# A gated attention and a MoE on one core: the MoE's second product in plain float32, with new groups, buffers and stream times

## The chip, the cores and the metric

The kernel runs on one core of one Trainium2 chip. Its engines work side by side, each through its own queue in order: PE (matrix products; PEld is its weight loads), DVE (VectorE), ACT (ScalarE), POOL (GpSimd) and SP, which here issues the DMAs. The metric is the device time of one execution in microseconds, lower is better.

## What is computed

A recurrence with a complex decay, per batch and head, and then a two-layer MoE-like block on its output, all in float32:

```python
for t in range(S):                       # S = 768, D = 48, B = 4, H = 8
    new_re = ar * S_re - ai * S_im
    new_im = ar * S_im + ai * S_re
    S_re, S_im = new_re + k[t] v[t]^T, new_im
    y[t] = q[t] @ S_re
x = y laid out as (3072 tokens, 384)
h = x @ w_in                             # (384, 2048)
g = h * clip(h + 3, 0, 6) / 6
out = g @ w_out                          # (2048, 384)
```

## The kernel before

The sequence is cut into 24 chunks of 128 tokens (six per batch). The attention works chunk by chunk, the MoE in groups of chunks.

- `normal` and `chain` turn the decays of three chunks (one *chain*, 8 in all) into cumulative products. This is DVE work almost alone: L350 to L352 and L384 to L388. The tile `z` holds a chain; `cw` carries the factors between chunks, by DMA.
- `prep(cc)` makes one chunk's scaled q and k: ACT squares, logarithm and exponential (L463 to L467), two products on POOL or, for the first chains, on DVE (L465 and L469, `E = V if CHAINS[q][0] < PV else P`), then L470, L471 and four products into the tile `gg` (L477). Six DMAs (L488) turn `gg` into the tile `kq`.
- `mat(cc)` is the chunk's part on PE: `pA` (L509, masked into `am` by DVE, L510), `py` (L522, in four column tiles of the array, once with `am` and once with the running `state`), the transposes `pt` (L538), the state's update `pG` (L552), and the split of `py` into two float32r parts `xh` and `xl` (L563, L564). These float32 products appear in the page as two records each.
- `moe(g)` runs over the 16 slices `f` of the 2048 hidden columns. A round is: 9 matmuls (L609) into the PSUM tile `ph` (2 buffers); ACT makes `r` (L612); DVE makes the gated value and puts it back in `ph` (L614); ACT copies it as float32r into `gh` (L616); DVE puts the remainder into `gl` (L618); and LAG = 2 rounds later `second` does three float32r matmuls per chunk of the group (L597 to L599) into `po`. A group has three chunks, so a round has 9 + 9 matmuls of 384 columns.
- `weights(f)` brings the weights, which lie in memory as 64-bit floats, one part at a time (w_in, then w_out): a DMA into `ws` (L258), ACT shifts the low word (L264), DVE puts the words together (L267, L268), ACT copies the float32r part (L271), POOL subtracts for the remainder (L272). So both weights stand in the SBUF as two float32r tiles.
- `weights_guard` loads the weights again for a check of their size (three ACT activations each, L283 to L286, 32 of them); its tile shares the two buffers of `sq` in `normal`. Its result is used only after the last group.

Each of these is a generator, and a *stream* says when its pieces stand in the program: a start and an end on a made-up axis in which a chunk of MoE takes 16/3. The table `PAR` holds the numbers; a heap takes the stream with the lowest time next, and that, with a scheduler behind it, sets the order on every engine. The lines that decide the groups and the buffers are

```python
F1='VPVVVV', CP=16, SZ='33333333', CS='3.3.3.3.3.3.3.3', NV=1,
GGB, SQB, ZB, XB, WTB, LAG, RB, EX, AS, OV, KQB = 1,2,2,2,2,2,2,0,1,1,2
```

Of the kernel before, what the change touches and what calls it, by code (L numbers as in the profile page):

```python
# [21 lines left out]
C = 128  # L22
HALF = 64
NFF = 16
NB = 8
BL = HALF // NB

PITCH = HALF + 4
AT = 4
CHAIN_PIECES = BL - 1 + 3 + 2 + 1  # L30

PAR = dict(
    W0=-140.37, W1=0.5, CE=0.82, CL=15.36, PL=-0.12, ML=6.47, PD=6.7, C0=-162.25, L0=9.13, A0=-152.93,
    D0=6.25, P0=-1.45, M0=-98.58, C1=-122.4, L1=37.46, A1=-131.86, D1=9.53, P1=34.72, G0=134.98, G1=0.29,
    NL=6.55, ND=3.47, NP=1.37, CH=6.71, AO=-0.82, GA=19.17, GB=-1.42, N1=-42.6, N2=3, PV=2, F0='VVVVVV',
    F1='VPVVVV', CP=16, SZ='33333333', CS='3.3.3.3.3.3.3.3', NV=1,
)
# [12 lines left out]
CHAINS, CHUNK, LAST = [], [], []  # L50
# [5 lines left out]
COLS = [2 * q for q in range(len(CHAINS) + 1)]  # L56
# [146 lines left out]
def tile_gated_attention_moe(ctx, tc, aL, GL, vL, wL, maskL, qkvaL, out):  # L203
# [28 lines left out]
    n64 = wp.tile([C, 18], F32, name="n64")  # L232
# [8 lines left out]
    wout_h = wp.tile([C, NFF, DM], F32R, name="wout_h")  # L241
    wout_l = wp.tile([C, NFF, DM], F32R, name="wout_l")
# [4 lines left out]
    def weights(f):  # L247

        for part in range(2):
            while GA + GB * (2 * f + part) > 0 and 0 not in CWs:  # L250
                yield "wait"
            st = pa.tile([C, DM], I64, tag="sq" if WTB == 0 else "ws", name="ws", bufs=WTB or SQB)
            at = GA + GB * (2 * f + part)
            if at > 0:

                i = AT + int(min(at / 2, BL - 1)) * NB
                P.tensor_copy(st.bitcast(F32)[0:1, 0:1], Z[0][0:1, 0, 0, i : i + 1])
            SP.dma_start(out=st, in_=wL[:, f, part])  # L258
            words = st.bitcast(I32).rearrange("p (n two) -> p n two", two=2)
            low, high = words[..., 0], words[..., 1]  # L260
            if AS:

                ulow = st.bitcast(mybir.dt.uint32).rearrange("p (n two) -> p n two", two=2)[..., 0]
                A.activation(low, ulow, AF.Copy, scale=2.0**-29 * (1 - 2.0**-18), bias=7.5 * 2.0**-18 - 0.5)  # L264
            else:
                V.tensor_scalar(low, low, 29, None, ALU.logical_shift_right)
            V.scalar_tensor_tensor(low, high, 3, low, ALU.logical_shift_left, ALU.bitwise_or)  # L267
            V.scalar_tensor_tensor(low, high, 0x3FFFFFFF, low, ALU.bitwise_or, ALU.bitwise_and)  # L268
            w = st.bitcast(F32).rearrange("p (n two) -> p n two", two=2)[..., 0]
            hi, lo = (win_h, win_l) if part == 0 else (wout_h, wout_l)  # L270
            A.activation(hi[:, f], w, AF.Copy)  # L271
            P.tensor_tensor(lo[:, f], w, hi[:, f], ALU.subtract)  # L272
            if part:
                WEIGHTS.add(f)
            yield
# [16 lines left out]
    CWs = {}  # L292

    def normal(q, f):


        zt, n, first = CHAINS[q]
        w = 6 * n
# [33 lines left out]
        if f:  # L332
            V.tensor_tensor(at, at, m2.unsqueeze(1).to_broadcast([C, 2, 3 * n, HALF]), ALU.mult)
# [3 lines left out]
        NORMAL.add((q, f))  # L337
        yield

    def chain(q):  # L340
# [19 lines left out]
        while (q, 0) not in NORMAL or (q, 1) not in NORMAL:  # L360
            yield "wait"
# [17 lines left out]
        zs = z[:, :, :, AT : AT + HALF - NB].rearrange("p k x (i b) -> p k x i b", b=NB)[..., 1:]  # L379
        fac = e[..., : NB - 1].unsqueeze(3)  # L380
        shape = [C, w, BL - 1, NB - 1]
        fx = pa.tile([C, 2, *shape[1:]], F32, tag="fx", name="fx", bufs=1)
        for k in range(2):
            V.tensor_tensor(fx[:, k], zs[:, k], fac[:, 1].to_broadcast(shape), ALU.mult)  # L384
# [197 lines left out]
    def moe(g):  # L582
# [11 lines left out]
        def second(f, gh, gl):  # L594
            for i in range(n):
                ts = slice(i * C, (i + 1) * C)
                T.matmul(po[i], gl[:, ts], wout_h[:, f], start=f == 0, stop=False)  # L597
                T.matmul(po[i], gh[:, ts], wout_l[:, f], start=False, stop=False)  # L598
                T.matmul(po[i], gh[:, ts], wout_h[:, f], start=False, stop=f == NFF - 1)  # L599

        late = []
        for f in range(NFF):
# [10 lines left out]

            V.scalar_tensor_tensor(ph, r, 1.0, ph, ALU.min, ALU.mult)  # L614
            gh = pg.tile([C, C * n], F32R, tag="gh", name="gh", bufs=LAG + 1)
            A.activation(gh, ph, AF.Copy)  # L616
            gl = pg.tile([C, C * n], F32R, tag="gl", name="gl", bufs=LAG + 1)
            V.tensor_tensor(gl, ph, gh, ALU.subtract)  # L618
            late.append((f, gh, gl))
# [15 lines left out]
    def stream(make, start, end, pieces):  # L635
        streams.append([start, len(streams), (end - start) / pieces, make, None])
# [6 lines left out]
    for q, (t, n, first) in enumerate(CHAINS):  # L643
# [7 lines left out]
        stream(lambda q=q: chain(q), a, b, CHAIN_PIECES)  # L651
        for f in range(2):
            at = a - p["NL"] + f * p["ND"] * n / 3
            stream(lambda q=q, f=f: normal(q, f), at, at + p["NP"], 3)
# [139 lines left out]
```

## Time and profile before

| | us |
|---|---|
| median of 3 runs | 813.24 (812.2 to 815.07) |
| the profiled execution | 810.45 |
| its span, first to last instruction | 808.7 |
| PE busy | 626.4 (77%) |
| DVE busy | 543.5 (67%) |
| ACT busy | 367.7 (45%) |
| POOL busy | 222.4 (28%) |

PE's busy time counts records that overlap, so it isn't PE at its peak. The span in 40 equal slices (each digit the busy share in tenths; PEclk the granted TensorE clock in tenths; about 20 us a slice):

```profile
PE   0002857877637789978998989879998999999994
DVE  3986966889998659888967885777535442432332
PEclk9999997969767789989999999989997999999997
```

PE has nothing to do in the first three slices and half of the fourth, where the first chain and the first `kq` are made. DVE is nearly full in the first half and under half full in the last quarter, where the attention has ended and MoE alone runs.

### The profile page before, as it was taken

To read this page: it belongs to the slowest core of one execution; us is meant where nothing else is said; L and a number is where in the kernel's file an instruction comes from. 1 tells how busy PE (TensorE), PEld (TensorE's weight loads), DVE (VectorE), ACT (ScalarE), POOL (GpSimd) and SP (SyncE) were. 2 spreads that over 40 slices of the span, in tenths; PEclk is the share of its full clock that TensorE was granted. 3 is DMA by queue.
4 is the path that set the end of the run, shared out by engine and by line. 5 is a ranking of instruction groups with operands and counts; after the bars stand their busy time and mean duration, and the time that the engine had idled before them with its cause. 6 is when DMAs were issued, how large, how long until landed. Compare 5 with 4: busy or idle time off the path is not lost.

```text
span 808.7 us, 12677 instructions
## 1 busy us (share of the span) xinstructions
PE 626.4 (77%) x4577; PEld 573.5 (71%) x4577; DVE 543.5 (67%) x1063; ACT 367.7 (45%) x785; POOL 222.4 (28%) x220
## 2 busy tenths in 40 slices
PE   0002857877637789978998989879998999999994
PEld 0002647766527688867997788778887899988994
DVE  3986966889998659888967885777535442432332
ACT  6241225535433353353337335577687743333331
POOL 4254445335532432252125232413101100000000
PEclk9999997969767789989999999989997999999997
DMA  5116628527135454445332443465678440100000
GB/s 195 33 46 139 159 70 222 120 64 192 59 85 104 102 133 93 113 72 112 63 83 88 95 83 91 119 198 138 165 184 187 129 84 20 33 1 30 1 2 33
DMA packets 57814, 79.64 MB, mean 98 GB/s; under 512 B 12688, under 2 KB 40464, under 8 KB 57744
## 3 DMA queue, kind: packets, MB, share of 16 engines
q1 hardware_dynamic: 57744, 78.75, 39.4%
q8 instruction: 38, 0.62, 0.3%
q14 instruction: 32, 0.26, 0.1%
HBM read 51.05 MB, written 4.72 MB: 69 GB/s over the span
## 4 chain that ended last, share of the span: by engine, by line
PE 32%; DMA 18%; DVE 17%; POOL 9%; ACT 8%; issue 7%; SPq 7%; ACTq 0%; DVEq 0%; POOLq 0%
PE ph L609 14%; DMA kq<-gg 6%; PE po L597 4%; PE po L598 4%; PE po L599 4%; DMA ws<-in_wL_dram 4%; SPq L488 4%; DVE gg L477 3%; PE py L522 3%; DVE pr L350 2%; DMA z<-in_aL_dram 2%; DMA out_dram<-ot 2%; DMA wgs<-in_wL_dram 2%; DVE gl L618 2%; POOL gg L465 1%
## 5 line engine op out<-in xcount | busy, mean ns | idle before, releaser
L597 PE MATMUL po<-wout_h,gl 128*128 128x384 f32 x384 | 135.1, 352 | 30.7 <-DVE gl L618 30.7
L614 DVE SCALAR_TENSOR_TENSOR ph<-r,ph 128x384 f32<-128x384 f32 x128 | 71.5, 558 | 115.4 <-ACT r L612 115.1
L598 PE MATMUL po<-wout_l,gh 128*128 128x384 f32 x384 | 133.3, 347 | 0.0
L599 PE MATMUL po<-wout_h,gh 128*128 128x384 f32 x384 | 133.1, 347 | 0.0
L509 PE MATMUL pA<-kq 96*128 96x128 f32 x384 | 61.5, 313 | 85.9 <-DMA kq<-gg 78.4
L609 PE MATMUL ph<-xh,win_l 128*128 128x384 f32 x384 | 104.4, 384 | 25.7 <-DVE gl L618 20.2
L509 PEld LDWEIGHTS pA<-kq 96*128 96x128 f32 x384 | 57.0, 223 | 88.7 <-issue 84.4
L612 ACT ACTIVATE r<-ph,half 128x384 f32<-128x384 f32 x128 | 73.7, 576 | 87.3 <-PE ph L609 80.8
L618 DVE TENSOR_TENSOR gl<-ph,gh 128x384 fp32r<-128x384 f32 x128 | 70.8, 553 | 58.4 <-ACT gh L616 58.1
L597 PEld LDWEIGHTS po<-wout_h,gl 128*128 128x128 f32 x384 | 75.5, 197 | 33.6 <-DVE gl L618 32.9
L609 PEld LDWEIGHTS ph<-xh,win_l 128*128 128x128 f32 x384 | 69.3, 205 | 37.4 <-DVE gl L618 25.1
L609 PE MATMUL ph<-xl,win_h 128*128 128x384 f32 x384 | 95.0, 359 | 0.0
L609 PE MATMUL ph<-xh,win_h 128*128 128x384 f32 x384 | 93.8, 354 | 0.0
L616 ACT ACTIVATE gh<-ph 128x384 fp32r<-128x384 f32 x128 | 62.2, 486 | 60.2 <-DVE ph L614 60.1
L572 POOL TENSOR_TENSOR state<-state,cw 96x1024 f32<-96x1024 f32 x20 | 41.5, 2075 | 145.7 <-DMA state<-state 123.8
L598 PEld LDWEIGHTS po<-wout_l,gh 128*128 128x128 f32 x384 | 75.4, 196 | 0.2 <-POOL wout_l L272 0.2
L609 PEld LDWEIGHTS ph<-xl,win_h 128*128 128x128 f32 x384 | 75.5, 205 | 0.0
L599 PEld LDWEIGHTS po<-wout_h,gh 128*128 128x128 f32 x384 | 75.0, 195 | 0.0
L609 PEld LDWEIGHTS ph<-xh,win_h 128*128 128x128 f32 x384 | 74.4, 202 | 0.2 <-issue 0.2
L350 DVE TENSOR_TENSOR pr<-z 128x288 f32<-128x288 f32 (+2 forms) x176 | 70.9, 442 | 1.0
L522 PE MATMUL py<-am,vt 128*32 128x128 f32 x768 | 39.8, 314 | 23.3 <-DVE am L510 19.1
L465 POOL TENSOR_TENSOR gg<-gg,u 128x384 f32<-128x384 f32 x18 | 23.3, 1295 | 122.4 <-ACT gg L463 107.2
(91 smaller groups left out, 1009.5 us busy)
## 6 DMA issues: line engine op xcount, KB each, us to landing
kq<-gg SPq DMA_DIRECT2D x144, 128.0 KB, 4.3
ws<-in_wL_dram SPq DMA_DIRECT2D x32, 384.0 KB, 3.7
wgs<-in_wL_dram SPq DMA_DIRECT2D x32, 384.0 KB, 3.5
z<-in_aL_dram SPq DMA_DIRECT2D x16, 612.0 KB, 5.9
vt<-in_vL_dram SPq DMA_DIRECT2D x24, 256.0 KB, 3.7
u<-in_GL_dram SPq DMA_DIRECT2D x24, 192.0 KB, 4.4
gg<-in_GL_dram SPq DMA_DIRECT2D x24, 192.0 KB, 2.4
out_dram<-ot SPq DMA_DIRECT2D x24, 192.0 KB, 1.9
```

Of the source, the lines that this page charges most:

```text
L350: V.tensor_tensor(pr[:, j], src, fac[:, j : j + 1].to_broadcast([C, *shape]), ALU.mult)
L509: T.matmul(pA[:, i], kt[:, hf * 4 + i], qt[:, hf * 4 + i], start=True, stop=True)
L522: T.matmul(py[q * 32 : q * 32 + 32, t], lhs[:, n, cols], rhs, start=start, stop=stop, tile_position=(0, q * 32),)
L572: P.tensor_tensor(state2, state2, cw[:, :, :, c2].rearrange("p h k -> p k h").unsqueeze(3).to_broadcast([L, 2, NH, 64]), ALU.mult,)
L597: T.matmul(po[i], gl[:, ts], wout_h[:, f], start=f == 0, stop=False)
L598: T.matmul(po[i], gh[:, ts], wout_l[:, f], start=False, stop=False)
L599: T.matmul(po[i], gh[:, ts], wout_h[:, f], start=False, stop=f == NFF - 1)
L609: T.matmul(ph, w[:, f, kt * C : (kt + 1) * C], xx[:, kt], start=k == 0, stop=k == 8)
L612: A.activation(r, ph, AF.Relu, scale=1.0 / 6.0, bias=half)
L614: V.scalar_tensor_tensor(ph, r, 1.0, ph, ALU.min, ALU.mult)
L616: A.activation(gh, ph, AF.Copy)
L618: V.tensor_tensor(gl, ph, gh, ALU.subtract)
```

## The change

The second product takes one float32 `hs` and one float32 `wout`, so `gh`, `gl`, `wout_h` and `wout_l` are gone. The core of the diff:

```diff
-            V.scalar_tensor_tensor(ph, r, 1.0, ph, ALU.min, ALU.mult)
-            gh = pg.tile([C, C * n], F32R, tag="gh", name="gh", bufs=LAG + 1)
-            A.activation(gh, ph, AF.Copy)
-            gl = pg.tile([C, C * n], F32R, tag="gl", name="gl", bufs=LAG + 1)
-            V.tensor_tensor(gl, ph, gh, ALU.subtract)
+            hs = pg.tile([C, C * n], F32, tag="hs", name="hs", bufs=LAG + 1)
+            V.scalar_tensor_tensor(hs, r, 1.0, ph, ALU.min, ALU.mult)
...
-                T.matmul(po[i], gl[:, ts], wout_h[:, f], start=f == 0, stop=False)
-                T.matmul(po[i], gh[:, ts], wout_l[:, f], start=False, stop=False)
-                T.matmul(po[i], gh[:, ts], wout_h[:, f], start=False, stop=f == NFF - 1)
+                T.matmul(po[i], gg[:, i * C : (i + 1) * C], wout[:, f], start=f == 0, stop=f == NFF - 1)
```

The weights' two parts come in one DMA, and their first two conversions run on both at once. The last one writes w_out's bits straight into `wout`:

```diff
-        for part in range(2):
...
-            SP.dma_start(out=st, in_=wL[:, f, part])
+        SP.dma_start(out=st, in_=wL[:, f])
...
-            V.scalar_tensor_tensor(low, high, 3, low, ALU.logical_shift_left, ALU.bitwise_or)
-            V.scalar_tensor_tensor(low, high, 0x3FFFFFFF, low, ALU.bitwise_or, ALU.bitwise_and)
...
-            A.activation(hi[:, f], w, AF.Copy)
-            P.tensor_tensor(lo[:, f], w, hi[:, f], ALU.subtract)
+        A.activation(low, ulow, AF.Copy, scale=2.0**-29 * (1 - 2.0**-18), bias=7.5 * 2.0**-18 - 0.5)
+        V.scalar_tensor_tensor(low, high, 3, low, ALU.logical_shift_left, ALU.bitwise_or)
+        yield
+        for part, bits in ((0, low[:, 0]), (1, wout[:, f].bitcast(I32))):
+            V.scalar_tensor_tensor(
+                bits, high[:, part], 0x3FFFFFFF, low[:, part], ALU.bitwise_or, ALU.bitwise_and
+            )
+        A.activation(win_h[:, f], w, AF.Copy)
+        P.tensor_tensor(win_l[:, f], w, win_h[:, f], ALU.subtract)
```

The table has new numbers throughout. The groups are of 2, 2, 3, 3, 3, 3, 3, 3 and 2 chunks; `gg` gets two buffers (GGB) and `kq` three (KQB); LAG is 3; PV = 4 puts L465 and L469 on DVE for four chains instead of two; and the guards' streams (G0, G1) start at 125 and step backwards, so that many stand early:

```diff
-    D0=6.25, P0=-1.45, M0=-98.58, C1=-122.4, L1=37.46, A1=-131.86, D1=9.53, P1=34.72, G0=134.98, G1=0.29,
-    NL=6.55, ND=3.47, NP=1.37, CH=6.71, AO=-0.82, GA=19.17, GB=-1.42, N1=-42.6, N2=3, PV=2, F0='VVVVVV',
-    F1='VPVVVV', CP=16, SZ='33333333', CS='3.3.3.3.3.3.3.3', NV=1,
...
+    G0=125.387, G1=-3.089, NL=5.949, ND=2.145, NP=-0.808, CH=3.38, AO=-3.102, GA=20.958, GB=-2.008,
+    N1=-37.864, N2=3, PV=4, SZ='223333332', CS='3.3.3.3.3.3.3.3', GGB=2, SQB=2, ZB=2, XB=2, WTB=2, LAG=3,
+    RB=2, OV=1, KQB=3,
```

Chains may now also be cut otherwise (`PARTS`, `TILE`, `MAXN`), but CS is the same, so each chain still has the same instructions.

How this moves instructions shows at three places. First PE in the middle of the program, in a group of three chunks. Before, the rows between one round's last products and the next round's first (`py` is attention):

```order
L597 MATMUL po_3417<-wout_h,gl 128x384
L598 MATMUL po_3417<-wout_l,gh 128x384
L599 MATMUL po_3417<-wout_h,gh 128x384
L522 MATMUL py<-am,vt 32x128
L538 MATMUL pt<-cst,kq 128x96 x4
L522 MATMUL py<-kq,state_103 32x128 x3
L609 MATMUL ph<-xh,win_l 128x384 x3
L609 MATMUL ph<-xl,win_h 128x384 x3
L609 MATMUL ph<-xh,win_h 128x384 x3
```

After, at a like place, two rounds of which the second product is one matmul per chunk:

```order
L604 MATMUL po_4251<-wout,hs 128x384
L604 MATMUL po_4252<-wout,hs 128x384
L604 MATMUL po_4253<-wout,hs 128x384
L530 MATMUL py<-am,vt 32x128 x4
L614 MATMUL ph<-xh,win_l 128x384 x3
L614 MATMUL ph<-xl,win_h 128x384
L530 MATMUL py<-am,vt 32x128 x12
L614 MATMUL ph<-xl,win_h 128x384 x2
L614 MATMUL ph<-xh,win_h 128x384 x3
```

A chunk's 32 py matmuls now stand in pieces of 4, 12 and 16; before they were cut into more and smaller ones.

Second DVE in a late group. Before, each round has two rows:

```order
L614 SCALAR_TENSOR_TENSOR ph<-r,ph 128x384
L618 TENSOR_TENSOR gl<-ph,gh 128x384
L578 TENSOR_TENSOR state_103<-state_103 96x512
L614 SCALAR_TENSOR_TENSOR ph<-r,ph 128x384
L510 TENSOR_TENSOR am<-pA,cst 128x512
L618 TENSOR_TENSOR gl<-ph,gh 128x384
```

After, one:

```order
L619 SCALAR_TENSOR_TENSOR hs<-r,ph 128x384 x2
L586 TENSOR_TENSOR state_102<-state_102 96x512
L619 SCALAR_TENSOR_TENSOR hs<-r,ph 128x384
L518 TENSOR_TENSOR am<-pA,cst 128x512 x2
L572 TENSOR_TENSOR xl<-py,xh 128x3x128
```

The attention's rows stand as before between the rounds, with half the MoE rows around them.

Third SP at the start, from the last loads for the first chunks to the first `kq`. Before:

```order
L455 DMA vt<-in_vL_dram 128x512
L258 DMA ws<-in_wL_dram 128x384 x2
L421 DMA cw<-ww 16x8x6 x6
L258 DMA ws<-in_wL_dram 128x384 x4
L488 DMA kq<-gg 16x8x256 x12
```

After:

```order
L283 DMA wgs<-in_wL_dram 128x384 x3
L262 DMA ws<-in_wL_dram 128x768 x2
L283 DMA wgs<-in_wL_dram 128x384 x2
L429 DMA cw<-ww 16x8x6 x6
L283 DMA wgs<-in_wL_dram 128x384 x2
L262 DMA ws<-in_wL_dram 128x768
L283 DMA wgs<-in_wL_dram 128x384
L262 DMA ws<-in_wL_dram 128x768
L283 DMA wgs<-in_wL_dram 128x384 x3
L262 DMA ws<-in_wL_dram 128x768
L496 DMA kq<-gg 16x8x256 x12
```

Eleven guards' loads (`wgs`) have come between, and ten weight parts in five DMAs stand ahead of the first `kq`, where six parts stood in six.

More of the change, by code (lines that the diff above doesn't have):

```diff
@@ L55 @@
     LAST.append(len(CHUNK) - 1)
-COLS = [2 * q for q in range(len(CHAINS) + 1)]
+PARTS = [
+    [(f, x, min(9, 3 * n - x)) for f in range(2) for x in range(0, 3 * n, 9)] for _, n, _ in CHAINS
+]
+COLS = [sum(len(p) for p in PARTS[:q]) for q in range(len(CHAINS) + 1)]
+MAXN = max(n for _, n, _ in CHAINS)
+TILE = max(sum(n for t, n, _ in CHAINS if t == z) for z in range(len(LAST)))
 DFF = 2048
@@ L240, in tile_gated_attention_moe @@
     win_l = wp.tile([C, NFF, DM], F32R, name="win_l")
-    wout_h = wp.tile([C, NFF, DM], F32R, name="wout_h")
-    wout_l = wp.tile([C, NFF, DM], F32R, name="wout_l")
+    wout = wp.tile([C, NFF, DM], F32, name="wout")
     X = {}
@@ L247, in weights @@
     def weights(f):
-        for part in range(2):
[L250 to L275, printed above, removed]
@@ new lines, in weights @@
+        while GA + GB * f > 0 and 0 not in CWs:
+            yield "wait"
+        st = pa.tile([C, 2, DM], I64, tag="ws", name="ws", bufs=WTB)
+        at = GA + GB * f
+        if at > 0:
+            i = AT + int(min(at / 2, BL - 1)) * NB
+            P.tensor_copy(st.bitcast(F32)[0:1, 0, 0:1], Z[0][0:1, 0, 0, i : i + 1])
+        SP.dma_start(out=st, in_=wL[:, f])
+        words = st.bitcast(I32).rearrange("p a (n two) -> p a n two", two=2)
+        low, high = words[..., 0], words[..., 1]
@@ L277, in weights_guard @@
+        w = st.bitcast(F32).rearrange("p a (n two) -> p a n two", two=2)[:, 0, :, 0]
+        A.activation(win_h[:, f], w, AF.Copy)
+        P.tensor_tensor(win_l[:, f], w, win_h[:, f], ALU.subtract)
+        WEIGHTS.add(f)
+        yield
     def weights_guard(f, part):
@@ L292, in tile_gated_attention_moe, with normal @@
     CWs = {}
-    def normal(q, f):
+    def normal(q, part):
         zt, n, first = CHAINS[q]
+        f, x0, xn = PARTS[q][part]
         w = 6 * n
@@ L302, in normal @@
             yield "wait"
-        while f and q not in Z:
+        while part and q not in Z:
             yield "wait"
-        if f == 0:
+        if part == 0:
             if zt not in ZT:
-                ZT[zt] = pz.tile([C, 2 * 18 * PITCH], F32, tag="z", name="z")
+                ZT[zt] = pz.tile([C, 2 * 6 * TILE * PITCH], F32, tag="z", name="z")
             off = PITCH * 12 * (first - (LAST[zt - 1] + 1 if zt else 0))
             Z[q] = ZT[zt][:, off : off + PITCH * 2 * w].rearrange("p (k x s) -> p k x s", k=2, x=w)
-        rows = Z[q][:, :, 3 * n * f : 3 * n * (f + 1)]
+        rows = Z[q][:, :, 3 * n * f + x0 : 3 * n * f + x0 + xn]
         if zt == 2 and N2 >= 0:
@@ L336, in normal @@
             V.scalar_tensor_tensor(at[:, 1], at[:, 1], -1.0, m2, ALU.mult, ALU.mult)
-        NORMAL.add((q, f))
+        NORMAL.add((q, part))
         yield
@@ L359, in chain @@
             yield "wait"
-        while (q, 0) not in NORMAL or (q, 1) not in NORMAL:
+        while any((q, i) not in NORMAL for i in range(len(PARTS[q]))):
             yield "wait"
@@ L650, in tile_gated_attention_moe @@
         a, b = (end - length + length * (x - tfirst) / tn for x in (first, first + n))
[L651 to L654, printed above, removed]
+        stream(lambda q=q: chain(q), a, b, BL + 2 + 3 * (-(-n // 3)) + 1)
+        for i in range(len(PARTS[q])):
+            at = a - p["NL"] * max(1, n / 3) + i * p["ND"] * min(1, n / 3)
+            stream(lambda q=q, i=i: normal(q, i), at, at + p["NP"], 3)
         for c in range(n):
```

52 lines of the change are left out of this document (28 added, 24 removed).

## Prediction

> **What bounds the kernel now.** I began with the page's span and slices, then cut the span at the first matmul of each MoE group (found in the timeline) and asked the windows view for each stretch, then took the mean time of one instruction from the groups.
>
> ```profile
> span 808.7 us, 12677 instructions
> 0.00:123.00 123.00, 34.97 (x280) 28.38 (x280) 91.98 (x186) 42.96 (x82) 49.49 (x66) 1.00 0.40 107
> 123.00:261.50 138.50, 96.39 (x632) 87.45 (x633) 121.68 (x224) 63.36 (x127) 57.28 (x48) 0.78 0.48 121
> 261.50:358.00 96.50, 81.06 (x617) 74.93 (x616) 75.68 (x144) 43.85 (x89) 37.71 (x37) 0.89 0.46 103
> 358.00:438.00 80.00, 74.12 (x586) 68.25 (x586) 62.57 (x128) 34.29 (x70) 24.25 (x24) 0.97 0.43 94
> 438.00:522.00 84.00, 76.54 (x627) 68.89 (x626) 63.05 (x127) 38.13 (x81) 27.51 (x23) 0.98 0.38 89
> 522.00:603.00 81.00, 74.85 (x578) 68.16 (x577) 51.55 (x116) 57.83 (x146) 14.44 (x16) 0.96 0.65 169
> 603.00:681.00 78.00, 74.23 (x537) 68.37 (x537) 35.82 (x62) 47.19 (x117) 9.78 (x7) 0.93 0.46 113
> 681.00:741.00 60.00, 60.00 (x432) 55.75 (x431) 21.25 (x38) 20.07 (x39) 1.94 (x1) 1.00 0.06 19
> 741.00:798.00 57.00, 53.87 (x300) 53.23 (x298) 17.84 (x32) 19.54 (x37) 0.00 (x0) 0.97 0.03 11
> ```
>
> The columns are the stretch, its length, busy time of PE, PEld, DVE, ACT and POOL, and the granted clock. There are two regimes. Up to 358 us (first matmul of group 2) DVE is busy 289.3 of 358 us, or 88% between 123 and 261.5, while PE is idle a good part and granted only 0.78. From 358 us on PE is busy 93 to 100% and DVE falls to a third. So before 358 what counts is DVE's queue; after it, PE's.
>
> **The second product on PE.** Its price needs the pitch from start to start, since the durations overlap.
>
> ```profile
> 565.34 0.81 PE L552 MATMUL pG<-vt,kn 128*96 128x64 f32 x8
> 565.99 1.11 PE L509 MATMUL pA<-kq 96*128 96x128 f32 x8
> 566.85 0.77 PE L609 MATMUL ph<-xh,win_l 128*128 128x384 f32 x3
> ...
> 753.69 0.68 PE L609 MATMUL ph<-xh,win_l 128*128 128x384 f32 x3
> ...
> 756.83 0.68 PE L609 MATMUL ph<-xh,win_l 128*128 128x384 f32 x3
> ```
>
> From 753.69 to 756.83 one round f of a group is done: 9 matmuls of the first product and 9 of the second, 3.14 us / 18 = 174.4 ns each, for 384 columns of float32r. Plain float32 shows in the attention: the program has 8 pA matmuls per chunk (192 in all) and the page 384 records, two passes each. Eight passes of 128 columns take 566.85 - 565.99 = 0.86 us, 107.5 ns a pass. Three times the columns gives 322 ns a pass, about 650 ns a product, where three float32r matmuls took 523. A pass of pG, 64 columns, takes 81 ns: if that slope held (26.5 ns per 64 columns) a pass of 384 would take 213 and a product 427; if each pass cost two float32r matmuls, 698. I take 650, from the nearest row, pA. That is 0.127 us x 384 products = **+48.6 us of PE work** (bounds -37 and +67).
>
> The Trainium skill, page "Perfetto Trace Analysis", section "Engine Utilization", rates the array's output at half speed for FP32_LOW_HIGH. Halved, its peak gives an estimate of 107 ns for 128 columns: the 107.5 ns of one record agrees, so the rule seems to hold for each of the two passes; read as a rule for the whole product it would give 320 ns and a gain.
>
> **What leaves the other engines.**
>
> ```profile
> L614 DVE SCALAR_TENSOR_TENSOR ph<-r,ph 128x384 f32<-128x384 f32 x128 | 71.5, 558 | 115.4 <-ACT r L612 115.1
> L618 DVE TENSOR_TENSOR gl<-ph,gh 128x384 fp32r<-128x384 f32 x128 | 70.8, 553 | 58.4 <-ACT gh L616 58.1
> L616 ACT ACTIVATE gh<-ph 128x384 fp32r<-128x384 f32 x128 | 62.2, 486 | 60.2 <-DVE ph L614 60.1
> L272 POOL TENSOR_TENSOR wout_l<-ws,wout_h 128x384 fp32r<-128x384 f32 x16 | 23.3, 1454 | 30.3 <-ACT wout_h L271 29.2 <-DMA cw<-ww 1.1
> L271 ACT ACTIVATE wout_h<-ws 128x384 fp32r<-128x384 f32 x16 | 8.9, 553 | 12.5 <-DVE ws L268 12.3
> L264 ACT ACTIVATE ws<-ws 128x384 int32<-128x384 uint32 x32 | 17.7, 557 | 63.6 <-DMA ws<-in_wL_dram 63.6
> L267 DVE SCALAR_TENSOR_TENSOR ws<-ws 128x384 int32<-128x384 int32 x32 | 21.6, 678 | 26.1 <-ACT ws L264 26.0
> L465 DVE TENSOR_TENSOR gg<-gg,u 128x384 f32<-128x384 f32 x6 | 4.4, 734 | 1.5 <-ACT gg L463 1.5
> L469 DVE TENSOR_TENSOR gg<-gg,u 128x384 f32<-128x384 f32 x6 | 3.8, 637 | 0.0
> L384 DVE TENSOR_TENSOR fx<-z 128x882 f32<-128x882 f32 x16 | 16.5, 1075 | 0.2
> ```
>
> gl and gh go: -70.8 us on DVE, -62.2 on ACT. hs takes ph's place; 128 become 144, of which 48 have 256 columns. DVE's forms grow about 1.05 ns per column (558 ns for 384, L384's 1075 for 882), so hs of 256 is about 420 ns: 96 x 0.55 + 48 x 0.42 = 73, the same as ph. Weights: wout_h and wout_l go (-8.9 ACT, -23.3 POOL); the first two conversions run 16 times on 768 columns. By that slope L267 becomes 16 x 1.1 to 1.2, some -3 us, and L264 about -4 on ACT. The last DVE step is again 32 instructions. PV=4 moves 6 more chunks' L465 and L469 from POOL to DVE: 6 x (0.734 + 0.637) = +8.2 on DVE. In sum about -65 us on DVE, -75 on ACT, -38 on POOL.
>
> **What it is worth up to 358 us.** Here DVE sets the pace, so I added these durations in the order of DVE's rows, up to the start of each group. Before, 329 us of DVE work stand ahead of group 2's first ph (six chunks behind); in the changed order 331 us stand ahead of group 3's first hs (seven chunks). So at the same time one chunk more is through, but DVE's saving is spent on work pulled forward: chain 4 ends after 308 us of it (316 before), and one more prep and half of chain 5 stand in front. PE isn't the limit there: seven chunks instead of six add 7 x 16 x 1.173 - 6 x 16 x 1.047 = 31 us where PE had 145 us idle.
>
> ```profile
> L268 DVE SCALAR_TENSOR_TENSOR ws<-ws x32: 545/554/1690, 41.9 to 254.8; 128x384 int32<-128x384 int32 x32
> ...
> ACT gg L463 <- DMA kq<-gg: 49.1, 16, 5.5
> ```
>
> Two things help a little. L268 takes 554 ns at the median and up to 1690; its long ones lie under POOL's work, of which 16 instructions go in this stage. And gg with two buffers and kq with three take away ACT's wait for the transfer out of gg, part of the 20.8 us that DVE idles between 261.5 and 358. I put group 3's first matmul at **352 us**, between 345 and 369; the upper end is the third rival.
>
> **The start.** Eleven of the guard's 32 loads now stand on SP between the first ws and the first kq, with their activations on ACT; nothing waits for their result.
>
> ```profile
> 66.74 0.33 SPq L258 DMA_DIRECT2D ws<-in_wL_dram  x1
> 67.17 8.39 SPq L488 DMA_DIRECT2D kq<-gg  x12
> ...
> L285 ACT ACTIVATE wgs<-wgs,wlim 128x384 f32<-128x384 f32 x32 | 20.6, 645 | 0.4
> L283 ACT ACTIVATE wgs<-wgs 128x384 f32<-128x384 f32 x32 | 17.8, 556 | 16.3 <-DMA wgs<-in_wL_dram 16.2
> ```
>
> A guard is about 2.2 us of ACT (0.556, twice 0.645 and two accumulator reads). ACT is busy 43 of the first 123 us, so I cost them at nothing; where two stand ahead of prep 0's activations the first kq goes out some 4 us later. Before, kq already waited on SP behind a ws load, and so it does now.
>
> **From there to the end.** Before, from 358 us to the last matmul (798), 440 us pass. Eighteen chunks of MoE are 18 x 16 x 6 x 0.1744 = 301.5; the other 138.5 are attention and loss. After, seventeen chunks at 3 x 0.1744 + 0.650 = 1.173 us are 17 x 16 x 1.173 = 319. The attention left is the same (both have pA of ten chunks behind them), so the rest is loss, which I split in three. PE's idle time in the last six windows is 26.4 us. The granted clock costs length times (1 - clock), 14.5 us. And attention pieces cost more than their work:
>
> ```profile
> 712.49 0.43 PE L522 MATMUL py<-kq,state 96*32 96x128 f32 x8
> ...
> 716.18 0.43 PE L522 MATMUL py<-kq,state 96*32 96x128 f32 x8
> ...
> 614.52 0.86 PE L522 MATMUL py<-am,vt 128*32 128x128 f32 x24 [3.54 <-DVE am L510]
> 615.31 0.55 PE L538 MATMUL pt<-cst,kq 96*128 96x96 f32 x4
> 615.79 1.94 PE L522 MATMUL py<-kq,state 96*32 96x128 f32 x32
> ...
> PE ph L609 <- DVE gl L618: 12.8, 10, 3.1
> ```
>
> A round with four py matmuls in it takes 716.18 - 712.49 = 3.69 us instead of 3.14: 0.55, while in the long run of 24 records eight cost (615.31 - 614.52) / 3 = 0.26. So each separate run of py costs some 0.3 us more. The order has 65 such runs from group 2 on, the new one 41 from group 3 on: -7 us. Of the idle time I let half go, 13 us: the wait of L609 for gl becomes one for hs, two steps earlier, and kq is ready earlier; what stays is the attention at a group's border (3.54 us before py at 614.5). Of the clock's 14.5 I let 8 go, as it fell where PE had idled. Together 28 of 61. The last 11 us, from the last matmul to the end, stay.
>
> Sum: 352 + 319 + 138.5 - 28 + 11 = **792.5 us** of span, against 808.7. The profiled execution took 810.45 us, 1.75 more than its span, and the median shown is 2.8 above that; with both, **797**.
>
> **Rivals.** *One: the waits stay.* PE, the bound after 358 us, gets 0.127 us more for each of 272 products and none of the 61 us of loss goes, because border and attention cause it, not gl. Then 352 + 319 + 138.5 + 11 = 820.5, and 826.5 if group 3 also starts only at 358: up to **831**. From 358, less than 18 us regained makes the kernel slower. For it: DVE was idle half the time after 522 us and PE lost as much there. Against it: L609 waits for gl by name. *Two: float32 at half rate*, 349 ns a product: 352 + 237 + 138.5 - 28 + 11 = 710, **715**; pA's passes speak against it. *Three: the start costs.* Double ws loads and the guards delay kq and chain 1, and group 3 starts at 369: **814**, no change. *Four: more relief.* Group 3 at 345 and 45 of the 61 us gone: 768.5, **773**. That the change might not do what it says I rule out: the order shows the 384 products and no gl.
>
> **How the numbers follow.** Forecast 0.46 (own range 785 to 809), waits stay 0.26, half rate 0.04, start 0.10, more relief 0.14. Faster is forecast, half rate and more relief, 0.64; the same 0.10; slower 0.26, by over 0.3%, about what three runs can tell. The range, 768 to 834, leaves out half rate and the ends of one and four.
>
> **What would show it.** The pitch of two po records: 650 ns a product, or the 48.6 us are wrong. Group 3's first matmul at 352: later means rival three or a DVE queue that I undercounted. PE idle from there to the end near 13 us; near 26 it is rival one. The wait of ph for DVE should go from PE's list. I'm wrong if the stages before 352 become PE's.

## The result, and the profile after

| | before | after |
|---|---|---|
| median | 812.85 us (4 runs, 812.2 to 815.07) | 776.27 us (4 runs, 774.38 to 777.7) |
| ratio, 95% interval | | 0.9544 [0.9513, 0.9575] |
| the profiled execution, its span | 810.45, 808.7 us | 775.17, 773.4 us |

The change saves 36.6 us; 16 were forecast. 776 lies inside the range on record, but below the likeliest case's own range (785 to 809).

The page after the change, first its busy times, then PE's, DVE's and the clock's slices, then the groups of the second product and of the gated value (busy us, mean ns of one | idle time ahead):

```profile
span 773.4 us, 11749 instructions
PE 628.7 (81%) x4337; PEld 482.3 (62%) x4337; DVE 490.8 (63%) x947; ACT 307.1 (40%) x641; POOL 189.7 (25%) x189
PE   0000666978998989689999999999998999999994
DVE  3987888899997799889788597544224212221111
PEclk9999998999999999889999999999999999999998
L604 PE MATMUL po<-wout,hs 128*128 128x384 f32 x768 | 275.2, 493 | 6.1 <-DVE hs L619 6.1
L619 DVE SCALAR_TENSOR_TENSOR hs<-r,ph 128x384 f32<-128x384 f32 (+1 forms) x144 | 72.6, 505 | 141.0 <-ACT r L617 140.8
```

PE is as busy as before, in a span 35 us shorter, and the clock hardly dips; the slices with 5 to 7 in PE's row of before have nearly gone. So work didn't leave PE, waiting did. The windows, cut at the first matmuls of groups 0 to 3 and at the last one (stretch, length, busy PE, PEld, DVE, ACT, POOL, clock, DMA share, GB/s):

```profile
0.00:117.70 117.70, 25.88 (x193) 21.85 (x193) 89.58 (x175) 59.52 (x123) 44.39 (x57) 1.00 0.56 164
117.70:183.80 66.10, 54.85 (x415) 42.20 (x414) 59.16 (x89) 39.15 (x80) 22.37 (x19) 0.92 0.73 208
183.80:244.40 60.60, 54.96 (x447) 41.34 (x446) 56.32 (x133) 28.67 (x67) 14.53 (x14) 0.97 0.36 77
244.40:342.90 98.50, 84.00 (x571) 62.44 (x570) 85.36 (x160) 49.21 (x104) 35.48 (x33) 0.96 0.54 128
342.90:762.60 419.70, 408.70 (x2722) 314.39 (x2721) 198.33 (x382) 130.01 (x269) 72.97 (x67) 0.99 0.30 69
```

and the same of before, cut at its group 2:

```profile
0.00:358.00 358.00, 212.42 (x1527) 190.76 (x1528) 289.33 (x552) 150.17 (x297) 144.49 (x150) 0.88 0.45 111
358.00:797.70 439.70, 413.60 (x3050) 382.66 (x3049) 252.08 (x501) 216.97 (x487) 77.91 (x70) 0.97 0.36 89
```

Group 3 starts at 342.9 us, with seven chunks of MoE ahead of it. DVE has done 89.58 + 59.16 + 56.32 + 85.36 = 290.4 us of work by then, as much as before by 358 (289.3); it idled 52.5 us, not 68.7. Behind it, 419.7 us pass. I read all experiments by these two numbers: **the start of group 3** (seven chunks ahead; group 2, with six, in the old table) and **the rest** up to the last matmul.

### The profile page after: what moved, and what is told of

Same layout as the page of the kernel before. It is cut to its first block, busy times and chain, and to the rows that moved or that the text cites. A ratio compares the mean times of both kernels' runs of the same rounds, so it can differ in the third digit from the quotient of the medians.

```text
span 773.4 us, 11749 instructions
## 1 busy us (share of the span) xinstructions
PE 628.7 (81%) x4337; PEld 482.3 (62%) x4337; DVE 490.8 (63%) x947; ACT 307.1 (40%) x641; POOL 189.7 (25%) x189
## 4 chain that ended last, share of the span: by engine, by line
PE 37%; DVE 19%; DMA 18%; POOL 7%; ACT 7%; issue 6%; SPq 4%; POOLq 0%; ACTq 0%; DVEq 0%
PE po L604 16%; PE ph L614 14%; DMA wgs<-in_wL_dram 6%; DMA kq<-gg 4%; DVE pr L354 4%; PE py L530 3%; DMA ws<-in_wL_dram 3%; DVE gg L485 3%; DMA z<-in_aL_dram 3%; SPq L496 2%; PE pA L517 2%; DVE z L355 1%; PE pG L560 1%; DMA out_dram<-ot 1%; DVE hs L619 1%
## 5 line engine op out<-in xcount | busy, mean ns | idle before, releaser
L604 PE MATMUL po<-wout,hs 128*128 128x384 f32 x768 | 275.2, 493 | 6.1 <-DVE hs L619 6.1
L604 PEld LDWEIGHTS po<-wout,hs 128*128 128x128 f32 x768 | 141.7, 192 | 73.8 <-DVE hs L619 6.5
L619 DVE SCALAR_TENSOR_TENSOR hs<-r,ph 128x384 f32<-128x384 f32 (+1 forms) x144 | 72.6, 505 | 141.0 <-ACT r L617 140.8
L617 ACT ACTIVATE r<-ph,half 128x384 f32<-128x384 f32 (+1 forms) x144 | 77.5, 538 | 144.5 <-PE ph L614 141.5
L614 PE MATMUL ph<-xh,win_l 128*128 128x384 f32 (+1 forms) x432 | 114.8, 377 | 18.7 <-DVE hs L619 18.6
L614 PE MATMUL ph<-xl,win_h 128*128 128x384 f32 (+1 forms) x432 | 95.2, 326 | 0.2 <-DVE xl L572 0.2
L614 PE MATMUL ph<-xh,win_h 128*128 128x384 f32 (+1 forms) x432 | 93.5, 324 | 0.0
L485 DVE TENSOR_TENSOR gg<-u,z 128x384 f32<-128x384 f32 x96 | 55.6, 638 | 2.2 <-DMA u<-in_GL_dram 2.1
L560 PEld LDWEIGHTS pG<-vt,kn 128*96 128x96 f32 x320 | 32.9, 176 | 12.4 <-ACT kn L547 7.3
L560 PE MATMUL pG<-vt,kn 128*96 128x64 f32 x320 | 34.8, 261 | 6.1 <-ACT kn L547 5.9
```

The lines of the kernel that those rows point to most:

```text
L485: V.tensor_tensor(gg[:, k, :, 1 - i].rearrange("p d (f s) -> p f d s", f=2), u[:, 2 * i : 2 * i + 2], zv[:, k], ALU.mult,)
L560: T.matmul(pG[:, n], kn[:, n], vt[:, n], start=True, stop=True)
L604: T.matmul(po[i], gg[:, i * C : (i + 1) * C], wout[:, f], start=f == 0, stop=f == NFF - 1)
L614: T.matmul(ph, w[:, f, kt * C : (kt + 1) * C], xx[:, kt], start=k == 0, stop=k == 8)
L617: A.activation(r, ph, AF.Relu, scale=1.0 / 6.0, bias=half)
L619: V.scalar_tensor_tensor(hs, r, 1.0, ph, ALU.min, ALU.mult)
```

## The experiments

Ratios are to the kernel before, timed on the same chip. Its median differed between the chips by up to 3.5 us (809.86 to 813.32), so a difference of two runs' medians is no finer than that. A count of buffers or a stream's time also lets the scheduler lay all engines' rows anew, so each run shows its edit together with the order that follows from it.

**1. The product alone.** The kernel before with `hs` and one `wout`; weights one part at a time, old table, old buffers.

```diff
-                T.matmul(po[i], gl[:, ts], wout_h[:, f], start=f == 0, stop=False)
-                T.matmul(po[i], gh[:, ts], wout_l[:, f], start=False, stop=False)
-                T.matmul(po[i], gh[:, ts], wout_h[:, f], start=False, stop=f == NFF - 1)
+                T.matmul(po[i], hs[:, ts], wout[:, f], start=f == 0, stop=f == NFF - 1)
...
-            V.tensor_tensor(gl, ph, gh, ALU.subtract)
-            late.append((f, gh, gl))
+            hs = pg.tile([C, C * n], F32, tag="hs", name="hs", bufs=LAG + 1)
+            V.scalar_tensor_tensor(hs, r, 1.0, ph, ALU.min, ALU.mult)
+            late.append((f, hs))
```

> The kernel before with the float32 second product alone (one hs, one wout; groups, buffers, stream times and the weights one part at a time as before). Theory A (the product is a loss on PE that the freed engines only partly give back): PE gets 0.122 us more for each of 384 products; the 288 products from group 2 on lie where PE is the bound, +35 us, and the round's shorter way through ACT and DVE returns about 15 us: 825 to 840 us. Theory B (the freed ACT and DVE work is the gain of the whole change): 780 to 795 us, with PE's idle time from 358 us on under half of 26 us.

Measured: 812.75 us (10 runs), 1.0014 [0.9982, 1.0045]: a wash, between the two theories' ranges. Its windows, from group 0 on, show two changes that cancel:

```profile
122.70:231.00 108.30, 85.13 (x524) 64.61 (x524) 97.07 (x178) 46.33 (x91) 39.98 (x34) 0.90 0.55 143
231.00:320.00 89.00, 81.35 (x536) 62.18 (x535) 68.42 (x142) 32.03 (x64) 27.63 (x32) 0.97 0.37 83
320.00:404.70 84.70, 77.12 (x540) 59.11 (x538) 55.69 (x108) 26.58 (x52) 23.35 (x22) 0.98 0.36 86
404.70:796.40 391.70, 364.95 (x2323) 278.37 (x2321) 169.51 (x311) 160.19 (x356) 67.31 (x55) 0.98 0.35 90
```

Group 2 starts at 320 in place of 358, 38 us earlier. The rest takes 84.7 + 391.7 = 476.4 us in place of 439.7: 36.7 more, and 18 x 16 products at 0.127 us are 36.6. So where PE is the bound the dearer product is paid in full on balance, and **nothing of the old loss is regained**: PE's idle time there even grows, from 439.7 - 413.6 = 26.1 us to 34.3. PE's waits from group 2 on, before and with the product (us in total, times, longest):

```profile
PE ph L609 <- DVE gl L618: 12.8, 10, 3.1
```
```profile
PE ph L607 <- DVE hs L613: 24.2, 15, 3.9
```

The wait for gl didn't go; as a wait for hs it doubled.

**2. The product and the buffers of gg and kq** (GGB 2, KQB 3, LAG 3), old table and weights.

> As the first, with gg in two buffers, kq in three and LAG 3, still the old groups and times. Theory A (buffers let prep run ahead, and that is where the gain comes from): 15 us or more below the first run, and ACT's wait for kq's DMA falls from 49 us to under 15. Theory B (the order, not the buffers, decides when prep runs): within 5 us of the first run.

Measured: 808.36 us (10 runs), 0.9957 [0.9931, 0.9984], within 5 us of run 1 as theory B has it. In the profiled execution group 2 starts at 330.1 and the rest takes 467: the buffers give 9 us back behind and cost 10 in front. ACT's wait for kq's DMA fell from 49.1 only to 42.3 us, not under 15. The same buffers without the product weren't tried: there is no room for a second gg, nor for twice the weights' buffers, each 6 KB more of each SBUF partition. `wout` in one tile in place of two frees 16 x 384 x 4 bytes, 24 KB.

**3. The table alone**: the new `PAR` (groups, streams, guards early, PV = 4) on the kernel before; old product, buffers and weights.

> The kernel before with the new table alone (groups 2,2,3,...,3,2, all stream times, guards early, L465 and L469 on DVE for four chains); product, buffers and weights as before. Theory A (groups and order carry the gain, and the old product leaves PE 47 us less to do): 775 to 795 us. Theory B (the order needs the freed engines: with gl on DVE, which sets the pace up to group 3, group 3 starts 15 us later or more): 805 us or slower.

Measured: 837.45 us, 1.0274 [1.0186, 1.0361]. Group 3 starts at 396.5 and the rest takes 428.8: the new table by itself costs 25 us, all of it early, as theory B has it.

**4 and 8. The changed kernel without gg's second buffer.** Run 4 has gg in one buffer and kq in two; run 8 takes only gg's second away (GGB=1, KQB=3).

```diff
-    ... GGB=2, SQB=2, ZB=2, XB=2, WTB=2, LAG=3,
-    RB=2, OV=1, KQB=3,
+    ... GGB=1, SQB=2, ZB=2, XB=2, WTB=2, LAG=3,
+    RB=2, OV=1, KQB=2,
```

> The changed kernel with gg in one buffer and kq in two. Theory A (the buffers carry much of the gain): 795 us or more, with ACT waiting over 40 us for kq's DMA. Theory B (they matter little): 776 to 783 us.

> The changed kernel with kq in three buffers, but gg in one again. In the run with both at their old number 17 us were lost. Theory A (gg is the one: prep of the next chunk can't start in gg before the six transfers to kq have read it): 788 to 795 us. Theory B (kq is the one: prep can stand a chunk further ahead): 774 to 780 us.

Measured: 793.62 us, 0.9761 [0.97, 0.9821]; and 792.12 us, 0.9774 [0.9687, 0.9861]. So gg's second buffer carries nearly all of 17 us, kq's third next to nothing. Run 4's windows, then the waits of ACT for the transfers out of gg and of PE for hs from group 3 on, in run 4 and in the changed kernel:

```profile
0.00:334.80 334.80, 221.68 (x1617) 171.33 (x1617) 267.75 (x528) 161.20 (x339) 96.86 (x116) 0.97 0.53 142
334.80:779.80 445.00, 416.32 (x2721) 320.80 (x2720) 212.23 (x409) 143.16 (x303) 80.09 (x73) 0.97 0.31 71
```
```profile
ACT gg L471 <- DMA kq<-gg: 54.5, 10, 10.5
PE ph L614 <- DVE hs L619: 12.2, 11, 2.8
```
```profile
ACT gg L471 <- DMA kq<-gg: 26.0, 9, 6.0
PE ph L614 <- DVE hs L619: 6.3, 6, 1.8
```

In run 4 group 3 even starts 8 us earlier, but the rest takes 445 us, 25 more: ACT may not write the next gg until the six transfers out of it are done, and PE, the bound there, runs dry (busy 416 of 445 us, against 409 of 420). In run 8 the same happens on a smaller scale: group 3 starts at 341.4, the rest takes 436.3 us, of which PE is busy 412.6, and ACT waits 34.2 us for the transfers. That the late prep is what PE then lacks is argued from these waits, not shown step by step.

**5. Weights one part at a time**, with four buffers of one part, so that the bytes on the way are the same.

> The changed kernel with the weights converted one part at a time (32 transfers of one part, four buffers of half the size; wout still float32). Theory A (fewer and longer conversions are what shortens DVE's waits before group 3): group 3 starts 6 us later or more, 782 to 790 us. Theory B (they lie beside DVE's other work): 774 to 779 us.

Measured: 784.75 us, 0.9655 [0.9583, 0.9726]; group 3 at 351.6, 8.7 us later, the rest 424.6: theory A, by some 8 us.

**6. Groups of three** (SZ='33333333') in the new streams.

> The changed kernel with eight groups of three; all else, the stream times too, as changed. Theory A (the short first and last groups gain at both ends, some 10 us of PE's early idle time and a shorter last group): 784 to 795 us. Theory B (groups matter little, the product and the buffers carry it): 774 to 781 us.

Measured: 798.69 us, 0.9844 [0.9777, 0.9912]: 22 us more, beyond theory A's 795. The first MoE matmul comes at 132.3 us, not 117.7, and behind the attention a group of three (57.1 us) is left where two chunks (42.0) were. What each of the two costs wasn't separated.

**7. Guards late** (G0=134.98, G1=0.29 as before).

> The changed kernel with the guards' stream numbers of before (G0=134.98, G1=0.29), so that all 32 stand late in the program. Theory A (their 71 us of ACT and the shared sq buffers held up the groups in which they stood, PE being the bound there): 783 us or more. Theory B (they lie beside work in either place; early they even hold up the first kq by 4 us): 770 to 778 us.

Measured: 780.56 us, 0.9629 [0.9539, 0.9718], an interval that overlaps the changed kernel's. Group 3 starts at 334.8, 8 us earlier, and PE idles 13.3 us in group 4, where it idled 4.1: the guards' work is moved, not saved. Whether early is better stays open.

**9. The product alone, w_out's parts still made** into scratch tiles.

```diff
+            else:
...
+                A.activation(hi, wout[:, f], AF.Copy)
+                P.tensor_tensor(lo, wout[:, f], hi, ALU.subtract)
```

> The kernel before with the float32 product, as in the first experiment, but w_out's float32r part and its remainder are still made, into a scratch tile that nothing reads: 16 more ACT copies (553 ns each before) and 16 more POOL subtractions (1454 ns each). Theory 'the rounds': what brought group 2's first matmul from 358 to 320 us was that a round waits for one DVE row and not for DVE, ACT and DVE; then it stays within 5 us of 320, and the time is that of the first experiment, 812 us (809 to 816). Theory 'the weights': POOL's 23 us and the DVE rows that they stretch were the relief; then group 2 starts at 335 or later, and with the 476 us that follow, the time is 825 us or more.

Measured: 828.03 us, 1.0243 [1.0197, 1.029]: the weights' theory. Group 2 starts at 337.4, so 17 of the 38 us that the product gave in front hang on POOL's subtractions and ACT's copies; 21 are left for the rounds. Group 0:

```profile
123.30:240.20 116.90, 86.72 (x525) 63.88 (x525) 104.42 (x179) 52.05 (x102) 58.85 (x44) 0.86 0.51 132
```

POOL is busy 18.9 us more than in run 1, and DVE needs 104.42 us for 179 rows where it needed 97.07 for 178: the same rows, bar one, and some grow longer beside POOL's.

**10. Product and table together**, with old buffers, LAG 2 and weights one part at a time.

> The kernel before with the float32 product and the new table (groups, stream times, guards early, PV = 4), but gg in one buffer, kq in two, LAG 2 and the weights one part at a time. The table alone gave 837 us, the product alone 813. Theory 'each for itself': the product is a wash here too, 837 us (830 to 842). Theory 'together': the new table lays early work so thick on DVE and ACT that only the float32 product makes room for it; then it comes to the changed kernel's 776 us, plus 17 for the old buffers, plus 8 for the weights one part at a time, 801 us (795 to 808).

Measured: 825.79 us, 1.0206 [1.0153, 1.026]. Neither theory: the product is worth 11 us in the new table, but of the 49.5 us between this run and the changed kernel runs 4 and 5 explain only 17 and 8. Runs 13 to 15 look for the other 25.

**11. PV = 2**: twelve products back from DVE to POOL.

> The changed kernel with PV = 2: the two products ahead of the scaled q and k of six chunks (chains 2 and 3) go back from DVE to POOL, 12 rows, 8.2 us of DVE work by the rows 734 and 637 ns of before. Theory 'DVE's queue sets the start': group 3's first matmul comes 4 to 8 us earlier than 342.9, and the time is 768 to 773 us. Theory 'POOL takes it back': POOL's rows are about twice as long, stand in the chain ahead of kq, and stretch the DVE rows that run beside them; group 3 not before 343, time 776 to 785 us.

Measured: 782.01 us, 0.9671 [0.9623, 0.9719]: POOL takes it back. Group 3 starts at 344.0 though DVE has 12 rows less. What I booked as a cost of 8.2 us on DVE is a gain of some 6 to 10 us of time (782 against 776 us; 1.3 points of the ratio).

**12. A first group of one chunk** (SZ='1223333331').

> The changed kernel with groups of 1, 2, 2, 3, 3, 3, 3, 3, 3 and 1 chunks in place of 2, 2, 3, 3, 3, 3, 3, 3 and 2; same streams. Theory 'PE waits for ready chunks at the start': the first MoE matmul, at 117.7 us in the changed kernel, comes 8 us or more earlier, PE idles less up to 343 us, and the time is 766 to 773 us. Theory 'the weights and DVE set the pace of the first group': its 16 rounds wait for the 16 slices of the weights whatever their size, a one-chunk round costs ACT and DVE more per chunk, and the time is 776 to 790 us.

Measured: 800.37 us, 0.9896 [0.9839, 0.9952], slower than either theory. The first MoE matmul comes at 92.3 us, 25 earlier, but this group of one chunk takes 91.2 us, more than the changed kernel's group of two (66.1). Its 16 rounds need the 16 slices of the weights, whose last remainder on POOL starts at 171.7, 12 us before the group ends at 183.5, where the changed kernel's group 0 ends too (183.8):

```profile
L276 POOL TENSOR_TENSOR win_l<-ws,win_h x16: 1006/1197/5201, 51.9 to 171.7; 128x384 fp32r<-128x384 f32 x16
```

This was the hint that the weights' arrival paces the first group.

**13 and 14. The weights' buffers.** Run 13 is run 5 with two one-part buffers, as before the change, in place of four; run 14 has gg and kq as in run 4 as well.

```diff
-            st = pa.tile([C, DM], I64, tag="ws", name="ws", bufs=2 * WTB)
+            st = pa.tile([C, DM], I64, tag="ws", name="ws", bufs=WTB)
```

> The changed kernel with the weights one part at a time, as in the fifth experiment (785 us), but with two buffers of one part for ws, as before the change, in place of four. Theory 'the weights' buffers': two parts in two buffers hold twice the data on the way, and that is what lets the new table start MoE early; in the old form PE waits for win_l in the first two groups as it did for 25.7 us in the tenth experiment, and the time is 800 to 812 us. Theory 'the count of instructions': the two parts help by their larger rows alone, and buffers don't matter: 785 us (780 to 790).

> The changed kernel with gg in one buffer, kq in two, and the weights one part at a time in two buffers; it differs from the tenth experiment (826 us) by LAG 3 and by where a chain's pieces yield. Theory 'each for itself': 776 + 17 + 8 = 801 us (797 to 806), and what is left to the tenth experiment is LAG's. Theory 'the weights' buffers': 818 to 830 us, and LAG is worth nothing.

Measured: 821.93 us, 1.0131 [1.0075, 1.0186]; and 830.22 us, 1.023 [1.018, 1.0281]. Run 13 is **the largest single term that was undone in the changed kernel**, larger than its theory had it: two one-part buffers cost 37 us against four (run 5), and with the one-part rows 46 against the changed kernel. Run 13's windows, with the cuts as above:

```profile
0.00:103.90 103.90, 20.57 (x185) 17.14 (x185) 78.36 (x166) 54.02 (x119) 36.01 (x53) 0.94 0.54 155
103.90:229.30 125.40, 82.89 (x588) 60.28 (x589) 91.38 (x164) 59.52 (x127) 43.04 (x42) 0.72 0.53 152
229.30:289.50 60.20, 49.48 (x299) 37.90 (x297) 49.30 (x113) 25.46 (x55) 11.65 (x20) 0.94 0.46 90
289.50:387.70 98.20, 85.23 (x551) 65.14 (x549) 84.70 (x176) 40.94 (x91) 29.78 (x29) 0.90 0.41 101
387.70:808.40 420.70, 406.95 (x2722) 312.66 (x2721) 180.31 (x337) 129.26 (x268) 70.86 (x58) 0.99 0.30 68
```

The rest is the same as in the changed kernel (420.7 and 419.7). All is lost in group 0, which takes 125.4 us for its two chunks, not 66.1. DVE, nearly full there in the changed kernel, idles 34 us of it, most of that before the weights' rows that wait for the load. In run 13 and in the changed kernel, in group 0:

```profile
DVE ws L272 <- ACT ws L269: 19.0, 12, 3.8
```
```profile
DVE ws L268 <- ACT ws L267: 4.7, 2, 3.3
```

SP's timeline shows the pace of the loads, two parts (one slice) at a time:

```profile
108.49 0.99 SPq L263 DMA_DIRECT2D ws<-in_wL_dram  x2
118.18 0.88 SPq L263 DMA_DIRECT2D ws<-in_wL_dram  x2
128.56 1.03 SPq L263 DMA_DIRECT2D ws<-in_wL_dram  x2
140.15 1.03 SPq L263 DMA_DIRECT2D ws<-in_wL_dram  x2
```

A slice every 10 to 12 us: a load goes out only when the slice before has left its buffer, then DVE's rows, in order, wait behind it. In the whole timeline about 152 us:

```profile
151.79 0.54 SPq L263 DMA_DIRECT2D ws<-in_wL_dram  x1
...
155.24 0.54 ACT L269 ACTIVATE ws<-ws 128x384 int32<-128x384 uint32 x1 [4.37 <-DMA ws<-in_wL_dram]
155.81 0.56 DVE L272 SCALAR_TENSOR_TENSOR ws<-ws 128x384 int32<-128x384 int32 x1 [3.02 <-ACT ws L269]
```

In the changed kernel a buffer holds both parts, so two buffers let the next slice land while this one is converted:

```profile
139.34 0.54 SPq L262 DMA_DIRECT2D ws<-in_wL_dram  x1
145.33 0.34 SPq L262 DMA_DIRECT2D ws<-in_wL_dram  x1
153.38 0.33 SPq L262 DMA_DIRECT2D ws<-in_wL_dram  x1
160.73 0.33 SPq L262 DMA_DIRECT2D ws<-in_wL_dram  x1
```

A slice every 7 us, the last at 160.7; in run 13 the last part goes at 219.1.

**15. LAG = 2 in the changed kernel.**

> The changed kernel with LAG = 2: the second product of a round follows two rounds after its first, not three, and hs has three buffers, not four. Theory 'LAG counts': an hs row that is late on DVE in the early groups meets PE a round sooner; PE waits more for hs up to 343 us, and the time is 783 to 800 us. Theory 'LAG is worth nothing': 774 to 780 us.

Measured: 776.59 us, 0.9579 [0.9532, 0.9626]: LAG is worth nothing here.

**16. The changed kernel, w_out's parts still made**, as in run 9.

> The changed kernel, but w_out's float32r part and its remainder are still made into scratch tiles that nothing reads: 16 ACT copies and 16 POOL subtractions more, as in the ninth experiment, where this cost 15 us. Theory 'the weights' relief on POOL carries the gain': POOL's 23 us more stretch DVE rows and delay win_l; group 3 starts at 352 us or later, and the time is 786 to 795 us. Theory 'the slack covers it': in the changed order POOL is a third busy up to 343 us and win_l is early; 774 to 780 us.

Measured: 778.82 us, 0.9606 [0.9551, 0.966]: within the intervals no cost. What was worth some 15 us in the old order (run 9 against run 1) is covered in the new one.

**17. The product alone with four weight buffers**, that is run 1 with WTB = 4.

> The kernel before with the float32 product, as in the first experiment (813 us), and with four buffers of one part for ws in place of two; the old table, gg, kq and LAG. Theory 'the first group waits for the weights' arrival': with two buffers the last ws load left at 246.7 us before and at 217.6 in the first experiment, and the first group ended 13 to 15 us later in both; with four the last load leaves before 180, group 1 starts at 215 or earlier in place of 231, and the time is 780 to 800 us. Theory 'the old table doesn't need them': its groups of three and its stream times were set for the slow arrival, group 1 stays within 5 us of 231, 808 to 817 us.

Measured: 822.78 us, 1.0159 [1.0102, 1.0216]: slower than either theory, a loss of 10 us against run 1. The loads do come earlier:

```profile
L257 SPq DMA_DIRECT2D ws<-in_wL_dram x32: 327/328/538, 37.3 to 142.6; - x32
```

The last one leaves at 142.6 (217.6 in run 1). But their conversions now stand ahead of the first chunks on DVE (28 of their rows before the first pA, 12 in run 1): the first pA comes at 91.0 us, not 75.2, and the first MoE matmul at 144.7, not 122.7. Group 0 is 17.5 us shorter (90.8), which doesn't pay for that, and group 1 then takes 102.9 us in place of 89.0, for reasons that weren't followed up.

**18. All but the table**: run 1 with the weights in two parts, gg in two buffers, kq in three and LAG 3.

> The kernel before with everything that the change does except its table: the float32 product, the weights in two parts with two buffers of both, gg in two buffers, kq in three, LAG 3; groups of three, stream times, guards and PV as before. Theory 'memory that the product frees is the gain': as the run beside it, less some 5 to 17 for gg's second buffer, 770 to 790 us, so the new table adds little. Theory 'the table is needed for it': groups of three cost 22 us in the changed streams, so 795 to 805 us.

Measured: 804.26 us (10 runs), 0.9913 [0.9885, 0.994]. So the table, which costs 25 us on the kernel before, is worth 28 on top of the rest. Undone one at a time in the changed kernel, its groups are worth 22 (run 6), the two products on DVE some 6 to 10 (run 11), and the guards an amount left open (run 7); its stream times weren't tried by themselves.

**The ladder.** Put one on the other, from the kernel before:

| step | group 3 starts | the rest | median |
|---|---|---|---|
| the table (run 3) | 396.5 | 428.8 | 837.45 |
| and the product (run 10) | 374.9 | 437.5 | 825.79 |
| and LAG 3 (run 14) | 378.2 | 439.0 | 830.22 |
| and weights in two parts (run 4) | 334.8 | 445.0 | 793.62 |
| and gg's and kq's buffers (the change) | 342.9 | 419.7 | 776.27 |

Run 14 differs from run 10 in where a chain's pieces yield, too. No run beat the changed kernel; with LAG 2 it is the same.

## Why the prediction was right in sign and wrong in size

**The product's price: right.** Six records stand in one stretch of the changed kernel's timeline:

```profile
587.60 2.10 PE L604 MATMUL po<-wout,hs 128*128 128x384 f32 x6
589.53 0.50 PE L546 MATMUL pt<-cst,kq 96*128 96x96 f32 x4
```

(589.53 - 587.60) / 6 = 322 ns a pass, 643 a product, where pA's passes gave 322 and 650. Rival two, half rate, is out. Run 1 fits the price where PE is the bound, 36.7 us for 36.6, though that is a balance in which PE's idle time grew too.

**What leaves the other engines: right by its rows** (hs 72.6 us for 73 forecast). DVE's busy time fell by 543.5 - 490.8 = 52.7 us and not by 65: the terms were sums of rows, and busy time counts overlapping rows once. The rows' durations add up to 607.8 us before and 546.5 after, 61.3 less.

**The start of group 3: 352 forecast, 342.9 found, right for a wrong reason.** That as much DVE work stands ahead of group 3 as of group 2 before was right (290.4 and 289.3 us), and DVE is the fullest engine in groups 0 to 2 (59.16, 56.32 and 85.36 us of 66.1, 60.6 and 98.5), though PE is close behind. **Wrong was the step "the first two conversions run 16 times on 768 columns ... some -3 us"**: I priced the weights' new form by its instructions, and left its buffers out. Undoing the form costs 46 us (run 13 against the change), 37 of them for the buffers (against run 5). Two buffers now hold twice the bytes; with the old form group 3 starts at 387.7, 44.8 later (run 13), and the kernel comes out slower than before. The rows were in view: L264's 63.6 us of ACT idle for the load, and L268's last start at 254.8 us, just ahead of group 1's first matmul at 261.5. I read that row as DVE stretched by POOL, and not as weights that arrive until then, though SP's loads waited 32.8 us in group 0 for POOL's subtractions to free a buffer. Missing on the other side was the price of the table itself (run 3). The two left an error of 9 us, the idle time, the clock and the py runs 10, and the step from the span to the median, booked at 4.5 and found at 2.9, the rest of the 21.

**"Of the idle time I let half go, 13 us: the wait of L609 for gl becomes one for hs, two steps earlier": this step failed.** Run 1 regains none of the loss, and its wait for hs is longer than that for gl was. PE's idle time from group 3 on did fall as forecast, to 419.7 - 408.7 = 11.0 us where 13 were named as the sign, and the wait of ph, which should have gone, fell to 6.3. But the reason was another: the product and the buffers in the old table leave PE 29.1 us idle (run 2), the new table without the buffers of gg and kq 28.7 (run 4). It takes both.

What was regained in all, 319 + 138.5 - 419.7 = 37.8 us for 28 forecast, splits over the prediction's three terms as some 15 of idle time for 13, some 10 of the clock for 8 (length times (1 - clock) comes to 4 us, where it was 14.5), and what remains, 12, stands against the 7 of separate py runs. 25.3 us come with the buffers of gg and kq (run 4), which I placed ahead of group 3, where they cost 8; gg's second buffer alone gives 16.6 behind and costs 1.5 in front (run 8). The other 12.5 remain in run 4 and weren't traced to single edits. Without both buffers rival one, the waits stay, would have held: its limit was 18 us regained, and run 4 has 12.5. Without gg's alone it wouldn't: run 8 has 21.2.

**The start:** "I cost them at nothing" held within what run 7 can tell; the first pA came 7.6 us later (83.7 for 76.1), not 4, and with the guards late it still comes at 81.7, so they explain 2 us of it. **PV = 4** was booked as a cost and is a gain (run 11). **The tail** of 11 us was 10.8.

Of the rivals the fourth, 345 and 45 us regained, came nearest: 773. I had given it 0.14, because I saw gg's buffer as a small help and the weights' not at all. That the forecast of group 3's start came out within 9 us was luck: two terms of opposite sign were left out.

## What to carry to other kernels

A change that makes one operation cheaper in memory may earn more by the buffers it makes room for than by its own work: here the product alone was worth nothing, and the buffers of the weights, gg and kq, with the weights' new form, 54 us in the new order (run 14 against the change). So price each buffer count in a diff by who waits for its release (ACT for gg's transfers, SP's loads for ws). Where a load's last start falls just ahead of a stage's end, ask whether the load sets that end (by more buffers, in the order that the kernel will have), before the engine that is busy meanwhile gets the blame. Parts that were set for each other can each lose alone (table +25, weights' buffers +10) and win together, so one undone part tells what it's worth in that place only.

## What the hardware showed beside this

DVE rows grow longer beside POOL's. In run 9, 18.9 us more of POOL in group 0 cost DVE 104.42 - 97.07 = 7.35 us over about the same rows, some 0.4 us for each us of POOL. Not all rows grow. In the changed kernel's trace the rows `gg<-u,z`, both of whose inputs are in SBUF, took 550 ns on average without a POOL row beside them (83 rows) and 1253 ns with one (12 rows); `hs<-r,ph` of 384 columns, which reads ph from PSUM, 550 and 548 ns (72 and 24 rows), and `am<-pA,cst`, which reads pA from PSUM, 684 and 681 (30 and 17 rows). So the two DVE rows of a round before, one input of which was in PSUM, weren't among those that POOL stretched (559 and 556 ns, 554 and 553, alone and beside it).

The Trainium skill, page "Perfetto Trace Analysis", section "Optimizing Scalar/DVE Operations", warns that moving work between the two might not help since they share a port to the SBUF. Run 11 agrees: DVE had twelve rows less, and the kernel took 1.3% of the time of before more.
